# A causal mixer and a routed mixture of experts on one core: weight preparation, one token fetch and a scratch tile in another order

## The chip, the cores and the metric

One core of a Trainium2 chip runs the whole kernel in one launch. The metric is the time on the device in microseconds (us): the median of three runs, which lay between 1354.47 and 1360.31. The core has TensorE (PE in the rows; its weight loads are PEld), VectorE (DVE), ScalarE (ACT), GpSimd (POOL) and SyncE (SP), which issues most of the transfers.

## The reference

The input x has 8 sequences of 3584 tokens with 192 values. Two steps are computed.

```python
# 1. causal mixing: 8 heads of 24 values, 7 taps, the taps' softmax per head
out[b, s, h, :] = sum_k softmax(weight[h])[k] * x_pad[b, s + k, h, :]
# 2. each of the 28672 mixed tokens goes to one of 8 experts
logits = normalised(x) @ normalised(expert_emb).T / tau
expert = argmax(logits);  gate = softmax(logits)[expert]
y = gate * (relu(x @ w1[expert]) @ w2[expert])     # 192 -> 1024 -> 192
```

## The kernel before

**Chunks.** The tokens are worked on in 16 chunks of 1792 (112 partitions by 16 tiles), numbered 0 to 15 here. `mix` (line 405) does a chunk's mixing: eight fp32 matmuls with a band matrix, each copied back by ScalarE, and then the sum of squares of each of the 16 token tiles, three of four on ScalarE (line 425) and one on VectorE (line 428). Both write the squares themselves, which nobody reads, into tiles with the tag "sq", of which there are two. `route` (line 448) splits the chunk into fp16 high and low parts (lines 457 to 464), transposes it, makes the logits (line 496), finds expert and rank of each token on VectorE, and lists 16 scatters that write the chunk's rows into a table in DRAM, `rows_d`, sorted by expert. Chunks 0 and 1 are transposed by TensorE; from chunk 2 on this is done by DMA, 16 transposes per chunk in SyncE's queue (line 597, issued by `turn`).

**Weights.** `prep_load` (line 273) asks for one expert's fp32 weights, into one of three staging places in turn. Two of them lie in the buffers "slot" and "hid", which the expert blocks use later, the third in the last two experts' own images inside "res". `prep_weights` (line 292) is a generator with four steps per expert. Step 0 squares W1 by a Gram pass on TensorE (line 318) and takes its diagonal's sum on VectorE (line 323, into an "sq" tile). Step 1 does W2: for experts 0 to 3 another Gram pass, from expert 4 (BEHIND) on a square on ScalarE (line 309) whose result is thrown into the W2 part of the expert's own image. Step 2 sums both (line 328) and makes powers of two as scales. Step 3 splits the scaled weights into a high fp16 part on ScalarE (line 337) and a low one on VectorE (line 341). After each step some steps of chunks' work are taken from `dispatch` (HEAD: 2 each from expert 4 on). After an expert's step 3 the staging place is asked for again, for the third expert behind.

**Expert blocks.** When the counts of enough chunks are known (PICK: 2, 3, 4, 6, 9, 12), `hand_out` selects blocks of tokens of one expert with `select` (line 630), a chain of small VectorE steps that uses one "sl_ge" tile. Behind chunk 1 these are seven blocks of 256 tokens. `fetch` (line 710) reads the block's place into a SyncE register and issues a transposing load of its tokens (line 721) and a small one of its row numbers and gates (line 724). A fetch waits for the scatters of all chunks that were listed when its block was selected. `copy_w1` and `copy_w2` (lines 703, 706) copy the block's expert from "res" to "slot"; `expert` (line 754) does the block: 40 matmuls into "h_ps" (line 776), relu and its low part (lines 780, 782) into "hid", 24 matmuls per 128 tokens into "o_ps" (line 799), the gate (line 804) and a scatter to the output (line 806).

**Order.** SyncE's instructions run in the order in which they are written (a manual schedule). On the other engines a list scheduler places the instructions when the program is built, by a modelled time and with the written order as priority; manual dependencies hold some behind others. A tile whose tag has all its buffers in use waits for one. Before the main loop of `run` stand, in this order: the eight experts' preparation with HEAD steps between; 14 steps of `dispatch` (PRE); the first `hand_out`; three fetches; 8 more steps. The main loop then writes expert blocks, with steps of `dispatch` between by a planner's costs and due times.

Of the kernel before, what the change touches and what calls it, by code (L numbers as in the profile page):

```python
# [12 lines left out]
F16 = mybir.dt.float16  # L13
F32 = mybir.dt.float32
BF16 = mybir.dt.bfloat16
I32 = mybir.dt.int32
AF = mybir.ActivationFunctionType
# [8 lines left out]
D = 192  # L26
E = 8
F = 1024
HALO = 16
TP = 112  # L30
# [5 lines left out]
W2 = 3 * F  # L36
# [3 lines left out]
NFC = F // 128  # L40
# [4 lines left out]
BEHIND = 4  # L45
HEAD = 9, 8, 9, 4, 2, 2, 2, 2
# [21 lines left out]
def _dep(tc, frm, to, sync=True):  # L68
    cls = mybir.DependencyClass.Sync if sync else mybir.DependencyClass.NoSync
    tc.add_manual_dep(  # L70
        frm, to, mybir.DependencyInfo(cls, mybir.DependencyReason.DATA),
        reason="routed rows are written before they are read",
    )


class _Moe:
# [217 lines left out]
    def prep_weights(self, e, st):  # L294
        nc = self.nc
        img = self.res[:, e * RES:(e + 1) * RES]


        st, sw = st
        sr, sv = (v.bitcast(BF16).rearrange("p (n k) -> p n k", k=2)[:, :, 1]  # L300
                  for v in (st, sw))
        acc = self.sp.tile([128, 2], F32, tag="w_acc", name="w_acc")
        for k, cols in enumerate(
                ([(sr, 128, i) for i in range(NFC)]
                 + [(sr, 64, i) for i in range(NFC, 2 * NFC)],
                 [(sv, 128, i) for i in range(NFC * D // 128)])):
            if k and e >= BEHIND:

                i = nc.scalar.activation(
                    out=img[:, W2:W2 + NFC * D], in_=sw, func=AF.Square,  # L310
                    accum_out=acc[:, k:k + 1]).ins
                _dep(self.tc, i, self.act[1].name, False)
                yield
                continue
            tr = self.ps("h", [128, 128], F32, "tr_ps")
            for n, (v, rows, i) in enumerate(cols):
                v = v[0:rows, i * 128:(i + 1) * 128]
                i = nc.tensor.matmul(out=tr, lhsT=v, rhs=v, start=(n == 0),
                                     stop=(n == len(cols) - 1)).ins
                if e >= BEHIND:  # L320
                    _dep(self.tc, i, self.turned.name, False)
            dg = self.sp.tile([128, D], F32, tag="sq", name="w_dg")[:, 0:128]
            nc.vector.scalar_tensor_tensor(
                out=dg, in0=tr, scalar=1.0, in1=self.idf, op0=ALU.mult,
                op1=ALU.mult, accum_out=acc[:, k:k + 1])
            yield
        ps = self.ps("h", [128, 2], F32, "n2_ps")
        nc.tensor.matmul(out=ps, lhsT=self.onef, rhs=acc, start=True, stop=True)
        s, si = self.pow2(ps, [128, 2], 198, "w_p")
        s1, s2 = s[:, 0:1], s[:, 1:2]  # L330
        nc.vector.tensor_tensor(out=img[:, WS:WS + 2].bitcast(F32), in0=si[:, 0:1],
                                in1=si[:, 1:2], op=ALU.mult)
        yield
        xb = img[:, 2 * F:W2]
        b = img[:, W2:WS].rearrange("p (c d) -> p c d", d=2 * D)
        s_b = sw.rearrange("p (c d) -> p c d", d=D)
        hi = [nc.scalar.activation(out=o, in_=i, func=AF.Copy, scale=m).ins
              for o, i, m in ((img[:, 0:F], st[:, 0:F], s1),
                              (xb[0:64, :], st[0:64, F:2 * F], s1[0:64]),
                              (b[:, :, 0:D], s_b, s2))]  # L340
        lo = [nc.vector.scalar_tensor_tensor(
            out=o, in0=i, scalar=m, in1=h, op0=ALU.mult, op1=ALU.subtract).ins
              for o, i, m, h in (
                  (img[:, F:2 * F], st[:, 0:F], s1, img[:, 0:F]),
                  (xb[64:128, :], st[0:64, F:2 * F], s1[0:64], xb[0:64, :]),
                  (b[:, :, D:], s_b, s2, b[:, :, 0:D]))]
        if e >= BEHIND - 1:
            for i in hi:
                _dep(self.tc, i, self.act[e >= BEHIND].name, False)
        for i in lo:  # L350
            if e >= BEHIND - 2:
                _dep(self.tc, i, self.dve[e >= BEHIND].name, False)
            elif e:
                _dep(self.tc, i, self.cut.name, False)
        yield


    def load_x(self, c):
# [46 lines left out]
    def mix(self, c, ring, first):  # L405
        nc, sp = self.nc, self.sp

        yield _Gate(self.asked[c] + LAND_X)
        xt = self.xts[c]
        xc = xt[0:TP]  # L410
        for h in range(H):
            ps = self.ps(ring, [TP, NT, G], F32, "conv_ps")
            i = nc.tensor.matmul(out=ps, lhsT=self.band[:, h, :],  # L413
                                 rhs=xt[:, :, h * G:(h + 1) * G],
                                 start=True, stop=True).ins
            self.behind(i)
            self.clk += STEPC
            nc.scalar.copy(out=xc[:, :, h * G:(h + 1) * G], in_=ps)  # L418
            yield 0.0, 0.46

        n2 = sp.tile([TP, NT], F32, tag="n2", name="n2")
        for t in range(NT):
            sq = sp.tile([128, D], F32, tag="sq", name="sq")[0:TP, :]
            if t % 4 < NACT:
                nc.scalar.activation(out=sq, in_=xc[:, t, :], func=AF.Square,  # L425
                                     accum_out=n2[:, t:t + 1])
            else:
                nc.vector.scalar_tensor_tensor(  # L428
                    out=sq, in0=xc[:, t, :], scalar=1.0, in1=xc[:, t, :],
                    op0=ALU.mult, op1=ALU.mult, accum_out=n2[:, t:t + 1])  # L430
            if t % 2:
                yield ((0.54, 0.0), (0.27, 0.35), (0.0, 0.7))[
                    (t % 4 < NACT) + ((t - 1) % 4 < NACT)]
        s, si = self.pow2(n2[:], [TP, NT], 195, "x_p")
        y = self.rsqrt(n2[:], [TP, NT], "x_r")
        f = sp.tile([TP, NT], F32, tag="f", name="f")
        nc.vector.tensor_tensor(out=f, in0=n2, in1=y, op=ALU.mult)
        nc.vector.scalar_tensor_tensor(out=f, in0=f, scalar=1e-6, in1=s,
                                       op0=ALU.add, op1=ALU.mult)
        nc.vector.reciprocal(out=f, in_=f)  # L440
        nc.vector.tensor_scalar(out=f, in0=f, scalar1=self.rtau[:, 0:1],
                                scalar2=None, op0=ALU.mult)

        yield 1.5, 0.0
        self.mixed[c] = xc, s, si, f
# [460 lines left out]
    def run(self):  # L906
# [11 lines left out]
        st = self.conv_taps(w)  # L918
# [2 lines left out]
        self.nc.gpsimd.memset(self.onef, 1.0)  # L921
        first = min(PICK)
        a, spent = self.dispatch(first, "h"), [0.0, 0.0]
        for e in range(E):
            for _ in self.prep_weights(e, st[e]):
                for _ in range(HEAD[e]):
                    v = next(a, None)
                    if e >= BEHIND:
                        spent = [s + t for s, t in zip(spent, v)]
            if e + 3 < E:  # L930
                st.append(self.prep_load(e + 3))
            while self.later:
                self.load_x(self.later.pop(0))
            if e == BEHIND - 1:
                for _ in a:
                    pass
                a = self.dispatch(first, "r")
        self.weights_in = True
        for n in PRE:
            for _ in range(n):  # L940
                spent = [s + t for s, t in zip(spent, next(a))]
            if not self.subs:
                self.hand_out(first)
                while self.ready < min(3, len(self.subs)):
                    self.fetch()
        self.gated = True
        live, due, done, out = next(a, None), [0.0, 0.0], False, 0.0
        while live or self.pend or not done or self.at < len(self.subs):
            if self.at < len(self.subs):
                for v in self.expert():  # L950
                    self.steer(spent)
                    out = min(1.0, out + self.pace)
# [4 lines left out]
                    while live and min(due) >= 0.0:  # L957
# [6 lines left out]
                        spent = [s + t for s, t in zip(spent, live)]  # L964
# [29 lines left out]
```

## Time and profile before

| | |
|---|---|
| median of three runs | 1357.72 us |
| profiled execution | 1352.22 us |
| its span, first to last instruction | 1350.1 us |
| TensorE busy | 1188.8 us (88%) |
| VectorE busy | 835.1 us (62%) |
| ScalarE busy | 583.3 us (43%) |
| GpSimd busy | 543.7 us (40%) |
| mean granted TensorE clock | 0.941 |

A row of a timeline names its start and length in us, the engine (SPq is SyncE's queue), the line, the operation, what it writes and reads, how many instructions are merged in it, and in brackets how long the engine stood idle ahead of it and what ended that. "Issue" and "remote" mean that the profile shows no instruction it waited for.

### The profile page before, as it was taken

The page shows a single profiled execution, that of the slowest core. Times are in us where ns is not written, and L with a number is a line of the kernel's source. Part 1 is how long each engine was busy: PE and PEld are TensorE (multiplying, and loading weights), DVE is VectorE, ACT ScalarE, POOL GpSimd, SP SyncE. Part 2 cuts the span into 40 slices and gives each one's busy share as a digit, 9 for nine tenths or more (in the row PEclk, how much of TensorE's full clock was granted, in tenths as well). Part 3 has the DMA queues.
Part 4 walks back from the last instruction along what each step waited for, and adds up shares of the span by engine and source line. Part 5 has one row for each costly group of instructions (what it writes and reads, how often), then busy time and mean ns, then how long its engine had stood idle before and what let it go on. Part 6 is the DMA issues. An engine that isn't in the chain of part 4 may idle for free. (4 is left out here: it accounts for less than half of the span.)

```text
span 1350.1 us, 28933 instructions
## 1 busy us (share of the span) xinstructions
PE 1188.8 (88%) x10572; PEld 911.7 (68%) x10572; DVE 835.1 (62%) x2207; ACT 583.3 (43%) x1343; POOL 543.7 (40%) x541
## 2 busy tenths in 40 slices
PE   5673789897889998999888999889999999999998
PEld 3542578686776676767556667567777777799787
DVE  3967657667776756676676564635445555467475
ACT  4957344444534544544444533324333333333332
POOL 0064252455444546456445555663222222223232
PEclk9666789999899998999998999989999999999999
DMA  9473534536357444565446344312212121113120
GB/s 262 125 221 91 118 76 105 129 94 132 97 128 147 98 115 106 124 138 130 117 119 145 83 103 84 97 63 57 51 37 52 42 52 43 36 40 66 33 45 22
DMA packets 273950, 129.10 MB, mean 96 GB/s; under 512 B 215774, under 2 KB 264285, under 8 KB 273808
## 3 DMA queue, kind: packets, MB, share of 16 engines
q1 hardware_dynamic: 250000, 80.39, 28.2%
q0 software_dynamic: 23808, 46.87, 11.8%
q8 instruction: 83, 1.36, 0.4%
q14 instruction: 59, 0.48, 0.1%
HBM read 38.35 MB, written 47.53 MB: 64 GB/s over the span
## 5 line engine op out<-in xcount | busy, mean ns | idle before, releaser
L799 PE MATMUL o_ps<-slot,hid 128*128 128x192 f16 x5544 | 516.8, 250 | 68.4 <-issue 39.8
L799 PEld LDWEIGHTS <-hid 128*128 128x128 f16 x5544 | 467.4, 100 | 118.7 <-issue 65.8
L776 PE MATMUL h_ps<-e_xT,slot 128*128 128x256 f16 (+2 forms) x2944 | 502.3, 304 | 13.0 <-issue 8.2
L806 POOL DMA_INDIRECT out_dram<-y,e_mt x231 | 259.2, 1122 | 510.4 <-ACT y L804 464.6
L776 PEld LDWEIGHTS <-slot 128*128 128x128 f16 x3680 | 326.5, 99 | 202.4 <-issue 31.2
L782 DVE SCALAR_TENSOR_TENSOR hid<-h_ps,hid 128x512 f16<-128x512 f32 x462 | 309.6, 687 | 194.5 <-ACT hid L780 152.6
L780 ACT ACTIVATE hid<-h_ps 128x512 f16<-128x512 f32 x462 | 267.1, 598 | 236.3 <-PE h_ps L776 166.1
L601 POOL DMA_INDIRECT rows_d<-rows,di x256 | 266.9, 1042 | 222.6 <-issue 84.0
L804 ACT ACTIVATE y<-o_ps,g 128x192 f32<-128x192 f32 x231 | 95.4, 420 | 337.7 <-PE o_ps L799 260.8
L776 PE MATMUL h_ps<-e_xf,slot 128*128 128x256 f16 (+2 forms) x736 | 211.3, 303 | 2.0 <-issue 2.0
L706 DVE COPY slot<-res 128x3074 f16 x88 | 85.9, 976 | 162.4 <-PE o_ps L799 103.3
L413 PE MATMUL conv_ps<-xt,band 128*112 128x384 f32 x256 | 112.2, 545 | 19.0 <-ACT xt L418 7.9
L418 ACT COPY xt<-conv_ps 112x384 f32<-112x384 f32 x128 | 60.1, 480 | 73.9 <-PE conv_ps L413 54.1
L459 ACT CAST rows<-xt 112x768 f16<-112x768 f32 x64 | 52.9, 830 | 75.7 <-DMA rows_d<-rows,di 35.0
L703 DVE COPY slot<-res 128x3072 f16 x88 | 83.7, 952 | 0.0
L496 PEld LDWEIGHTS <-xT 128*112 128x112 f16 x768 | 58.7, 149 | 33.7 <-DMA xT<-rows 20.8
L496 PE MATMUL lg_ps<-ma,xT 128*112 128x16 f16 x512 | 57.9, 204 | 21.3 <-DMA xT<-rows 19.1
L413 PEld LDWEIGHTS conv_ps<-xt,band 128*112 128x112 f32 x256 | 43.2, 195 | 41.1 <-issue 20.5
L461 DVE TENSOR_TENSOR rows<-xt,rows 112x512 f16<-112x512 f32 x64 | 44.0, 687 | 40.5 <-ACT rows L459 30.9
L425 ACT ACTIVATE sq<-xt 112x192 f32<-112x192 f32 x192 | 67.8, 356 | 2.7 <-DVE sq L428 1.7
L457 DVE TENSOR_TENSOR xt<-xt,x_p_s 112x768 f32<-112x768 f32 x64 | 58.3, 952 | 0.2
L496 PE MATMUL lg_ps<-mb,xT 128*112 128x16 f16 x256 | 47.2, 206 | 1.9 <-ACT xT L492 1.4
(163 smaller groups left out, 528.7 us busy)
## 6 DMA issues: line engine op xcount, KB each, us to landing
xt<-in_dram SPq DMA_DIRECT2D x39, 384.0 KB
xt<-in_dram SPq DMA_DIRECT2D x3, 1440.0 KB
rows_d<-rows,di POOLq DMA_INDIRECT x256
res<-in_dram SPq DMA_DIRECT2D x5, 768.0 KB
out_dram<-y,e_mt POOLq DMA_INDIRECT x231
xT<-rows SPq DMA_TRANSPOSE x224
xt<-in_dram SPq DMA_DIRECT2D x2, 1536.0 KB
hid<-in_dram SPq DMA_DIRECT2D x3, 768.0 KB
```

The lines of the kernel that those rows point to most:

```text
L413: i = nc.tensor.matmul(out=ps, lhsT=self.band[:, h, :], rhs=xt[:, :, h * G:(h + 1) * G], start=True, stop=True).ins
L425: nc.scalar.activation(out=sq, in_=xc[:, t, :], func=AF.Square, accum_out=n2[:, t:t + 1])
L496: i = nc.tensor.matmul(out=lg[:, g * GX + a, :], lhsT=xT[:, a, k, :], rhs=self.mb if k == 1 else self.ma, start=(k == 0), stop=(k == 2)).ins
L601: i = self.nc.gpsimd.indirect_dma_start(out=self.rows_d[:, :], out_offset=bass.IndirectOffsetOnAxis(ap=idx, axis=0), in_=src, in_offset=No ...
L703: self.under(nc.vector.tensor_copy(out=self.slot[:, 0:W2], in_=v).ins)
L706: self.nc.vector.tensor_copy(out=self.slot[:, W2:], in_=self.res[:, bass.ds(self.we + W2, RES - W2)])
L776: self.mm = nc.tensor.matmul(out=ps[:, c, :], lhsT=w1(o, b + c), rhs=xk[k], start=(i == 0), stop=(i == 4)).ins
L780: self.step = nc.scalar.activation(out=hh[:, b:b + m, :], in_=ps, func=AF.Relu).ins
L782: self.low = nc.vector.scalar_tensor_tensor(out=hl[:, b:b + m, :], in0=ps, scalar=0.0, in1=hh[:, b:b + m, :], op0=ALU.max, op1=ALU.subtrac ...
L799: self.mm = nc.tensor.matmul(out=o, lhsT=h[:, c, q], rhs=w2[:, c, k:k + D], start=(c + i == 0), stop=(c == NFC - 1 and i == 2)).ins
L804: self.step = nc.scalar.activation(out=y, in_=o, func=AF.Copy, scale=g[:, a:a + 1]).ins
L806: i = nc.gpsimd.indirect_dma_start(out=self.out[:, :], out_offset=bass.IndirectOffsetOnAxis(ap=mt[:, a, 0:1], axis=0), in_=y, in_offset=No ...
```

## The change

The preparation's steps are put into a list and sorted: steps 0 and 1 of experts 5, 6 and 7 now stand ahead of step 3 of the expert before. Each still has its HEAD steps of `dispatch` behind it, so their number is the same, and so is the number of loads and their order. The first `hand_out` and one fetch stand ahead of the 14 steps, a second fetch ahead of the 8, and the third is written by the first `expert`. The square of W2 throws its result into a tile with the tag "xT" of the pool that block tokens use (three buffers). The products that VectorE throws away (the Gram diagonals and its share of the chunks' squares) go into a tile with the selection's tag "sl_ge"; the "sq" tiles are left to ScalarE.

```diff
@@ -307,7 +307,8 @@
             if k and e >= BEHIND:
 
                 i = nc.scalar.activation(
-                    out=img[:, W2:W2 + NFC * D], in_=sw, func=AF.Square,
+                    out=self.ep.tile([128, 3 * 512], F16, tag="xT", name="w_sq"),
+                    in_=sw, func=AF.Square,
                     accum_out=acc[:, k:k + 1]).ins
                 _dep(self.tc, i, self.act[1].name, False)
                 yield
@@ -319,7 +320,7 @@
                                      stop=(n == len(cols) - 1)).ins
                 if e >= BEHIND:
                     _dep(self.tc, i, self.turned.name, False)
-            dg = self.sp.tile([128, D], F32, tag="sq", name="w_dg")[:, 0:128]
+            dg = self.waste(128, 128)
             nc.vector.scalar_tensor_tensor(
                 out=dg, in0=tr, scalar=1.0, in1=self.idf, op0=ALU.mult,
                 op1=ALU.mult, accum_out=acc[:, k:k + 1])
@@ -355,6 +356,10 @@
         yield
 
 
+    def waste(self, p, n):
+        return self.lp.tile([128, D], F32, tag="sl_ge", name="waste")[0:p, 0:n]
+
+
     def load_x(self, c):
         nc = self.nc
         b, r0 = c // self.per_b, (c % self.per_b) * CT
@@ -420,13 +425,14 @@
 
         n2 = sp.tile([TP, NT], F32, tag="n2", name="n2")
         for t in range(NT):
-            sq = sp.tile([128, D], F32, tag="sq", name="sq")[0:TP, :]
             if t % 4 < NACT:
+                sq = sp.tile([128, D], F32, tag="sq", name="sq")[0:TP, :]
                 nc.scalar.activation(out=sq, in_=xc[:, t, :], func=AF.Square,
                                      accum_out=n2[:, t:t + 1])
             else:
                 nc.vector.scalar_tensor_tensor(
-                    out=sq, in0=xc[:, t, :], scalar=1.0, in1=xc[:, t, :],
+                    out=self.waste(TP, D), in0=xc[:, t, :], scalar=1.0,
+                    in1=xc[:, t, :],
                     op0=ALU.mult, op1=ALU.mult, accum_out=n2[:, t:t + 1])
             if t % 2:
                 yield ((0.54, 0.0), (0.27, 0.35), (0.0, 0.7))[
@@ -921,12 +927,20 @@
         self.nc.gpsimd.memset(self.onef, 1.0)
         first = min(PICK)
         a, spent = self.dispatch(first, "h"), [0.0, 0.0]
-        for e in range(E):
-            for _ in self.prep_weights(e, st[e]):
-                for _ in range(HEAD[e]):
-                    v = next(a, None)
-                    if e >= BEHIND:
-                        spent = [s + t for s, t in zip(spent, v)]
+        beats = [(e, k) for e in range(E) for k in range(4)]
+        beats.sort(key=lambda v: 4 * v[0] - 1.7 + v[1] * 0.3
+                   if v[0] > BEHIND and v[1] < 2 else 4 * v[0] + v[1])
+        gens = {}
+        for e, k in beats:
+            if not k:
+                gens[e] = self.prep_weights(e, st[e])
+            next(gens[e])
+            for _ in range(HEAD[e]):
+                v = next(a, None)
+                if e >= BEHIND:
+                    spent = [s + t for s, t in zip(spent, v)]
+            if k < 3:
+                continue
             if e + 3 < E:
                 st.append(self.prep_load(e + 3))
             while self.later:
@@ -936,13 +950,12 @@
                     pass
                 a = self.dispatch(first, "r")
         self.weights_in = True
+        self.hand_out(first)
         for n in PRE:
+            if self.ready < len(self.subs):
+                self.fetch()
             for _ in range(n):
                 spent = [s + t for s, t in zip(spent, next(a))]
-            if not self.subs:
-                self.hand_out(first)
-                while self.ready < min(3, len(self.subs)):
-                    self.fetch()
         self.gated = True
         live, due, done, out = next(a, None), [0.0, 0.0], False, 0.0
         while live or self.pend or not done or self.at < len(self.subs):
```

## Rows read from the trace of the kernel before

**Rows 1.** Four stretches: length, busy us per engine (instructions), clock, DMA share, GB/s.

```profile
100.00:120.00 20.00, 8.06 (x30) 4.15 (x30) 10.92 (x38) 13.35 (x44) 14.24 (x14) 0.78 0.33 104
120.00:150.00 30.00, 11.32 (x61) 8.07 (x62) 25.31 (x71) 16.05 (x27) 0.25 (x1) 0.50 0.48 106
...
165.00:175.00 10.00, 2.94 (x16) 1.25 (x15) 2.09 (x4) 0.60 (x1) 6.05 (x7) 0.70 0.66 148
175.00:250.00 75.00, 72.22 (x685) 62.60 (x684) 52.43 (x133) 34.15 (x83) 27.52 (x26) 0.95 0.36 85
```

**Rows 2.** TensorE's timeline, 100 to 192 us.

```profile
105.94 6.00 PE L413 MATMUL conv_ps<-xt,band 128*112 128x384 f32 x10 [4.93 <-ACT xt L418]
...
139.16 2.87 PE L413 MATMUL conv_ps<-xt,band 128*112 128x384 f32 x4 [6.24 <-DMA xt<-in_dram]
...
149.11 3.31 PE L776 MATMUL h_ps<-e_xT,slot 128*128 128x256 f16 x16 [2.51 <-DMA e_xT<-rows_d]
...
158.89 0.82 PE L776 MATMUL h_ps<-e_xT,slot 128*128 128x256 f16 x6
...
177.08 1.06 PE L776 MATMUL h_ps<-e_xT,slot 128*128 128x256 f16 x4
...
189.78 0.60 PE L776 MATMUL h_ps<-e_xT,slot 128*128 128x256 f16 x4
```

**Rows 3.** SyncE's queue, 120 to 170 us.

```profile
120.09 11.18 SPq L597 DMA_TRANSPOSE xT<-rows  x8
...
131.95 0.42 SPq L375 DMA_DIRECT2D xt<-in_dram  x1
132.49 12.07 SPq L597 DMA_TRANSPOSE xT<-rows  x8
146.06 1.23 SPq L721 DMA_TRANSPOSE e_xT<-rows_d  x1
...
151.31 1.22 SPq L721 DMA_TRANSPOSE e_xT<-rows_d  x1
...
164.33 0.51 SPq L375 DMA_DIRECT2D xt<-in_dram  x1
166.04 1.25 SPq L721 DMA_TRANSPOSE e_xT<-rows_d  x1
```

**Rows 4.** VectorE's timeline, 94 to 145 us.

```profile
96.28 0.20 DVE L654 TENSOR_TENSOR sl_ge<-sl_a,jf 1x56 f32<-1x56 f32 x1
...
103.96 0.16 DVE L677 CAST sel<-sl_ro 1x7 int32<-1x7 f32 x1
...
118.79 0.29 DVE L323 SCALAR_TENSOR_TENSOR w_dg<-tr_ps,idf 128x128 f32<-128x128 f32 x1 [3.36 <-remote]
...
121.11 0.35 DVE L428 SCALAR_TENSOR_TENSOR sq<-xt 112x192 f32<-112x192 f32 x1
...
128.23 0.35 DVE L428 SCALAR_TENSOR_TENSOR sq<-xt 112x192 f32<-112x192 f32 x1
...
142.24 0.95 DVE L703 COPY slot<-res 128x3072 f16 x1
```

**Rows 5.** Groups by line, 83 to 150 us: VectorE's split passes of two experts.

```profile
L341 DVE SCALAR_TENSOR_TENSOR res<-hid,w_p_s,res 128x1024 f16<-128x1024 f32 (+2 forms) x6 | 8.7, 1454 | 0.1
```

**Rows 6.** ScalarE's timeline: the squares of W2 of experts 6 and 7.

```profile
103.26 1.48 ACT L309 ACTIVATE res<-res 128x1536 f16<-128x1536 f32 x1 [3.20 <-DVE res L341]
...
128.26 1.48 ACT L309 ACTIVATE res<-hid 128x1536 f16<-128x1536 f32 x1 [0.94 <-DVE res L341]
```

**Rows 7.** GpSimd's timeline: the last scatter of chunk 1.

```profile
116.78 0.94 POOL L601 DMA_INDIRECT rows_d<-rows,di  x1 [0.30 <-issue]
```

**Rows 8.** Waits of VectorE, 150 to 900 us: total, times, longest.

```profile
DVE sq L428 <- ACT sq L425: 23.6, 17, 6.3
```

**Rows 9.** Waits of TensorE, 150 to 900 us.

```profile
PE o_ps L799 <- DVE hid L782: 6.9, 11, 2.1
PE lg_ps L496 <- DMA xT<-rows: 2.3, 3, 1.3
```

## The prediction, written before the changed kernel ran

> **What bounds the kernel now.** I read the busy time by stretch first [rows 1]. From 175 us on TensorE sets the time: 72.2 of 75 us busy in 175 to 250, and the page's slices behind 850 us show it at 9 tenths. Not so at the front: from 100 to 150 TensorE works 19.4 of 50 us, at a granted clock of 0.78 and then 0.50 (its lower level, 1.2 GHz), while VectorE works 10.9 of 20 and then 25.3 of 30. From 165 to 175 nobody works (TensorE 2.9 of 10), with the DMA engines 66% busy.
>
> Next TensorE's timeline, for what ends its idle time at the front [rows 2]: the mixing matmuls wait 4.93 us for ScalarE, the mixing of chunk 4 6.24 us for its x, and the first expert block starts at 149.11 after 2.51 us for its own tokens. Block 0 then takes 9.8 us (149.11 to 158.89), block 1 18.2 (to 177.08), block 2 12.7 (to 189.78).
>
> Why the tokens come so late is seen in SyncE's queue, which runs in the order written [rows 3]: 16 transposes of chunk 2 with a load of x between them occupy it from 120.09 to 144.56, and only then stand the three fetches, the first at 146.06 and the last at 151.31. Data is there 3.05 us after an issue (146.06 to 149.11). The slot copy of block 0's weights needs every weight in its place; it starts at 142.24, behind the last split pass of expert 7 [rows 4]. So two things hold block 0, at 142 and at 149, and the queue is the later.
>
> **The change, part by part.**
>
> *Squares and Gram passes ahead of the split.* Before, the square of W2 threw its result into the expert's own image. For experts 6 and 7 that memory is another expert's staging, so ScalarE's queue stood 3.20 us at 103.26 and 0.94 us at 128.26 until VectorE's split had read it [rows 6]. Behind the first of these stood the copies that TensorE waited 4.93 us for. The diagonal of expert 7's Gram pass waited 3.36 us on VectorE, until 118.79 [rows 4]; the passes of ScalarE's squares just ahead of it use the same two "sq" tiles, and I take that as the reason. Nothing is added: the same Gram passes, squares of 1.48 us and three VectorE split passes of 1.454 on the mean, 4.4 us per expert [rows 5], stand in another order. What is moved is VectorE's: in 100 to 120 it idles 9.1 of 20 us [rows 1]. Earliest end of expert 7's split: behind expert 5's last pass, which let ScalarE go on at 103.26, two splits of 4.4, eight squares of 0.35 and an estimated 20 small steps of 0.16 (as the one at 103.96), 118. Latest: where it is, 142.3. I take 121, nearer to the early end, because the waits that held its links, 3.36 and 0.94 us and all that queued behind them, are the ones that go.
>
> What is pushed back for it? Chunk 2's subtractions, whose first rows started the transposes at 120.09. VectorE has 8.8 us of splits more ahead of them and 9.1 us of idle time to put them in. I leave their start where it is, at 120 (bounds 117, if only the 3.36 us goes, and 126, if half of the idle time stays).
>
> *The first fetch ahead of the transposes.* It needs the selection, which was complete at 103.96 [rows 4], and the scatters of chunks 0 and 1, whose last issue is at 116.78 and lasts 0.94 [rows 7]; their landing isn't in the rows. With the 3 us that a token fetch takes as the upper bound and nothing as the lower, the fetch is issued between 117.7 and 121; I take 120.5. Its tokens are there at 123.5, behind expert 7's split, and block 0 runs from 124 to 134 in time that TensorE idles now. A fetch takes 2.6 us of the queue (two in 146.06 to 151.31), so the transposes start at 123 instead of 120.09 and last the same 24.5 us, to 147.5. Fetch 1 goes out at 149.0 (the step from last transpose to fetch was 1.5), its tokens are there at 152, and block 1 starts at 152 where it started at 158.89: 6.9 us sooner, not the 25 by which block 0 is.
>
> Fetch 2 now stands behind chunk 3's eight transposes and the load of chunk 5. That stretch of queue took 14.7 us (151.31 to 166.04), so it goes out at 163.7. Block 1 gets block 0's old 9.8 us and ends at 162. Block 2 starts at 167 to 171 (3 us behind the issue, or when the load of 1.5 MB is through, which took 7.2 us at 131.95 to 139.16); I take 169, against 177.08: 8 us. In the old run the load of chunk 5 at 164.33 fell on block 1's second half: in 165 to 175 TensorE, VectorE and ScalarE all stood [rows 1], and block 1 took 8.4 us more than block 0. It now falls where TensorE waits for fetch 2 anyway.
>
> Order in one queue decides between 167 and 171, and no row here shows it: tokens fetched right behind the load of chunk 5 were not used until long after. The Trainium skill, DMA: Bandwidth & Descriptors, section "Two DMAs through the same engine are not ordered", says that within one queue of an engine descriptors start in order; by it block 2 would start at 171 and the gain would be 6, without it 10.
>
> Block 0 paid for a cold TensorE: its first 16 matmuls took 3.31 us after a stretch at clock 0.50. The same four matmuls took 1.06 us at 177.08, behind the standstill, and 0.60 at full clock, at 189.78 [rows 2], so 16 cold ones lose about 1.8. The change opens a second such gap, from 134 to 152, so block 1 pays 1.8 us too; that is in the 9.8 I gave it. The Trainium skill, TensorE: Matmul & The Clock Gate, section "Part 1: The HAM clock gate", says that throttled is the default and activity releases it, which speaks against running one block alone; if block 1 kept its clock, the gain would be 1.8 more.
>
> *Own tile for VectorE's squares.* In 150 to 900 VectorE stood 23.6 us in 17 pieces for ScalarE's squares, and TensorE 6.9 us for VectorE's hid [rows 8, 9]. These share only little: bounds 0 and 6.9, and I take 1, since VectorE is busy 70% of 175 to 250 and catches up. The tile is the selection's "sl_ge", of which there is one, so squares and selections now follow one another in it. All of it is VectorE's own, which needs no wait; but a selection can't run before squares written ahead of it.
>
> *Sum.* 8 from the front and 1 from the tile. From 175 on the work is the same, TensorE-bound, and what waits there is not for tokens or transposes (2.3 us in 750 for the logits [rows 9], none named for block tokens), so I carry it to the end: 1352.2 - 9 = 1343 for a profiled execution. The profiled one before lies 5.5 us under the median of its runs (1357.72), so the time is 1348.5. Likeliest case's own range: gains of 4 to 15, 1343 to 1354.
>
> **Rivals.**
>
> *A, larger:* transposes start at 117, since the diagonal's wait goes, and block 1 starts at 149 with its full clock; block 2 follows at 164. Gain 13 at block 2 and up to 4 more from VectorE's squares, 17: 1341. For it: all three waits are long and removed. Against it: the scatters hold the first fetch to 117.7 at the least.
>
> *B, nothing:* block 0 isn't taken out of its place. The order on TensorE is fixed when the program is built; chunk 4's mixing stood there in front of ready logits and made them wait 6.24 us. If block 0's matmuls stand behind the logits of chunk 2 again, it starts at 148 to 150, block 1 follows at 158, and fetch 2, 12 us later than before, holds block 2 to 169 or more, so what is left is the stretch around 165: gain 0 to 4, 1356. For it: that row. Against it: the tokens are there 20 us before the last logits.
>
> *C, slower:* the first fetch blocks SyncE. The selection can't take its one tile before chunk 3's squares; three of them were written ahead of it and ran between 121.11 and 128.23 [rows 4]. If they stay there, the selection ends at 128.6 plus the 7.7 us from its comparison to its result (96.28 to 103.96), the fetch is issued at 137 and the transposes start at 139.5, 19 us late. By the steps above block 1 then starts at 168.5, fetch 2 goes out at 180, and block 2 starts at 183 to 187, 8 us later than before: 1366. Block 2 is no later than before as long as the first fetch leaves by 129; from there each us costs one. Against it: these squares move up with expert 6's and 7's steps.
>
> **How the numbers follow.** Forecast 0.47, A 0.14, B 0.24, C 0.15. What a measurement here can tell from no change is about 0.5%, 6.8 us: faster means under 1350.9. Of the forecast I count 0.37 there and 0.10 within; A wholly faster; B 0.01 faster, 0.21 within and 0.02 slower; C 0.02 within and 0.13 slower. Faster 0.52, same 0.33, slower 0.15. Range: down to 1337 for what lies beyond A's low end, and up to 1361, which leaves C's worst out.
>
> **What would show it.** Right: the first token fetch ahead of the first row transpose, near 120; ScalarE's second W2 square without a wait; expert 7's split over by 125; block 0 starting near 124 and block 1 near 152, with TensorE at half clock between; block 2 near 169. Wrong: SyncE idle at its first fetch until after 125 (C); block 0 at 148 or later (B); block 2 at 169 but the distance lost by 900 us, which would mean that the stalls in the middle are not fixed costs.

## The result: 1.1% slower, and where the time went

The changed kernel took 1369.53 us (median of 6 runs, 1367.16 to 1374.21) beside 1355.9 for the one before on the same chip: ratio 1.0108, 95% interval 1.0081 to 1.0134. Its profiled execution took 1370.0 us, span 1368.1, granted clock 0.932. The forecast was 1348.5.

SyncE's queue of the changed kernel, 120 to 176 us (start, duration, instruction, count), to be held against [rows 3]:

```profile
130.04 1.34 SPq L727 DMA_TRANSPOSE e_xT<-rows_d  x1
...
132.15 11.45 SPq L603 DMA_TRANSPOSE xT<-rows  x8
...
144.81 11.76 SPq L603 DMA_TRANSPOSE xT<-rows  x8
157.37 1.24 SPq L727 DMA_TRANSPOSE e_xT<-rows_d  x1
...
159.98 1.25 SPq L727 DMA_TRANSPOSE e_xT<-rows_d  x1
...
162.04 12.02 SPq L603 DMA_TRANSPOSE xT<-rows  x8
174.18 0.51 SPq L380 DMA_DIRECT2D xt<-in_dram  x1
175.57 1.27 SPq L727 DMA_TRANSPOSE e_xT<-rows_d  x1
```

The first fetch leaves at 130.04, not 120.5, and everything written behind it on SyncE is late: chunk 2's transposes start 12.06 us later (132.15 against 120.09), and the fetch behind chunk 3's transposes and the load of x leaves at 175.57 instead of 166.04.

VectorE's timeline of the changed kernel, 113 to 130 us, against [rows 4]; the ends of the lines say what each writes and reads:

```profile
117.21 2.59 DVE L342 SCALAR_TENSOR_TENSOR res<-hid,w_p_s,res 128x1024 f16<-128x1024 f32 x2
...
119.92 1.81 DVE L342 SCALAR_TENSOR_TENSOR res<-hid,w_p_s,res 128x1536 f16<-128x1536 f32 x1
121.65 0.68 DVE L467 TENSOR_TENSOR rows<-xt,rows 112x512 f16<-112x512 f32 x1
...
126.28 0.36 DVE L433 SCALAR_TENSOR_TENSOR waste<-xt 112x192 f32<-112x192 f32 x1
...
126.71 0.11 DVE L659 MEMSET sl_ge<- 1x63 f32 x1
...
126.86 0.20 DVE L660 TENSOR_TENSOR sl_ge<-sl_a,jf 1x56 f32<-1x56 f32 x1
...
128.70 0.10 DVE L683 CAST sel<-sl_ro 1x7 int32<-1x7 f32 x1
```

The reader sees two things. The selection's comparison, at 96.28 before, starts at 126.86, directly behind the third of chunk 3's squares (126.28) in the same one tile; the selection is complete at 128.70 and the fetch leaves 1.34 us later. And expert 7's split (117.21 to 121.7) now stands ahead of chunk 2's first subtraction (121.65), which frees the first transposes. That subtraction was at 119.01 before, so of the 12.06 us the rows are 2.64, the selection 7.31 (the transposes began 1.08 behind the first subtraction before, so they could have begun at 122.73; the fetch leaves at 130.04) and the fetch itself 2.11 (130.04 to 132.15). The scatters are not what held the fetch: the last of them is issued at 119.61, and in e10 below a fetch leaves 2.6 us behind that point.

TensorE's timeline of the changed kernel, and its busy time in the stretches of [rows 1] (columns as there):

```profile
133.19 3.57 PE L782 MATMUL h_ps<-e_xT,slot 128*128 128x256 f16 x16 [14.21 <-DMA e_xT<-rows_d]
...
160.45 3.57 PE L782 MATMUL h_ps<-e_xT,slot 128*128 128x256 f16 x16 [2.41 <-DMA e_xT<-rows_d]
...
184.38 0.82 PE L805 MATMUL o_ps<-slot,hid 128*128 128x192 f16 x4 [5.52 <-issue]
```

```profile
120.00:150.00 30.00, 12.06 (x112) 10.35 (x112) 25.10 (x80) 11.79 (x36) 3.59 (x5) 0.71 0.33 82
165.00:175.00 10.00, 10.00 (x107) 9.38 (x106) 8.57 (x29) 4.33 (x8) 2.56 (x3) 1.00 0.45 77
175.00:250.00 75.00, 59.68 (x569) 50.80 (x567) 43.65 (x113) 28.05 (x71) 29.66 (x30) 0.89 0.40 93
```

Block 0 does run out of its place, at 133.19 instead of 149.11, but block 1 starts at 160.45 instead of 158.89. The standstill that was at 165 to 175 is now behind the later load of x: TensorE's pieces put down to "issue" add to 13.2 us from 178 to 194 (5.52 the longest), where they were 7.0 from 165 to 175 before. In 175 to 250 TensorE is busy 12.5 us less than before [rows 1].

To follow the loss I use the start of VectorE's gate step, one per expert block (`g<-e_mt,slot`). After minus before, in us: block 0 -12.0, block 1 +0.8, block 2 -5.5, block 3 +8.4, block 6 +8.2, block 36 +10.1, block 42 +19.8, last block +18.2. So 8 us are lost by block 3, and some 10 more between blocks 36 and 42. In that second stretch TensorE's waits for VectorE add to 9.7 us after and 2.9 before, and it is busy 5.1 us longer; what makes VectorE late there stays open.

### The profile page after: what moved, and what is told of

The parts are those of the page before. It is cut to its first block, busy times and chain, and to the rows that moved or that the text cites. A ratio compares the mean times of both kernels' runs of the same rounds, so it can differ in the third digit from the quotient of the medians.

```text
span 1368.1 us, 28953 instructions
## 1 busy us (share of the span) xinstructions
PE 1199.3 (88%) x10572; PEld 914.6 (67%) x10572; DVE 840.0 (61%) x2207; ACT 578.4 (42%) x1343; POOL 550.1 (40%) x541
## 5 line engine op out<-in xcount | busy, mean ns | idle before, releaser
L607 POOL DMA_INDIRECT rows_d<-rows,di x256 | 272.9, 1066 | 213.3 <-issue 103.1
L418 PE MATMUL conv_ps<-xt,band 128*112 128x384 f32 x256 | 117.7, 567 | 17.3 <-ACT xt L423 7.4
```

The costliest lines, as they stand in the source:

```text
L418: i = nc.tensor.matmul(out=ps, lhsT=self.band[:, h, :], rhs=xt[:, :, h * G:(h + 1) * G], start=True, stop=True).ins
L607: i = self.nc.gpsimd.indirect_dma_start(out=self.rows_d[:, :], out_offset=bass.IndirectOffsetOnAxis(ap=idx, axis=0), in_=src, in_offset=No ...
```

## Experiments

They ran on several chips. The kernel before took 1344.7 us beside e1 to e4 and 1267 us beside all the others; each result is the ratio to the kernel before on the same chip, with its 95% interval. "Selection" is the start of its last step, "transposes" that of chunk 2's first one. T is the theory "the late selection holds SyncE".

**e1: a tile of its own for VectorE's squares** (half precision; nothing else uses it), else as after.

```diff
-        return self.lp.tile([128, D], F32, tag="sl_ge", name="waste")[0:p, 0:n]
+        return self.lp.tile([128, D], F16, tag="waste", name="waste")[0:p, 0:n]
```

> The changed kernel, but VectorE's thrown-away products go to an fp16 tile with a tag of its own instead of the selection's tile. Theory T (the selection stands behind chunk 3's squares in the one shared tile, so the first fetch left at 130.0 and held SyncE's transposes by 12 us): selection over by 112, first fetch issued at 118 to 122, transposes from 121 to 124, block 1 at 151 to 154; total 0.988 to 1.000 of before. Rival R1 (the fetch ahead of the transposes is itself the loss: queue time, cold TensorE, fetch 2 behind the load): block 1 early, but the total stays over 1.005. Rival R2 (the splits put ahead push chunk 2's rows back): transposes not before 126, total 1.004 to 1.010. Rival R3 (VectorE's squares without the shared sq tiles cost the middle): front 6 us early, 10 us lost between 600 and 900, total 1.003 to 1.010.

Measured 1.0041 (1.0012 to 1.0070). The selection is complete at 104.32 and the fetch leaves at 122.30, yet the transposes start only at 126.98. Both signs of R2 come true (transposes not before 126, 1.004 to 1.010). VectorE shows why: chunk 2's first subtraction stands behind the copy of the first fetched tokens, and that copy waits for them.

```profile
125.41 0.46 DVE L749 COPY e_xf<-e_xT 64x256 f16<-64x256 f16 x2 [6.86 <-DMA e_xT<-rows_d]
125.88 0.69 DVE L467 TENSOR_TENSOR rows<-xt,rows 112x512 f16<-112x512 f32 x1
```

The ratio is about 0.7% lower than the change's, each known to 0.3%, but the time isn't under before, so T isn't all.

**e2: the squares back in the two shared "sq" tiles**, else as after.

```diff
-        return self.lp.tile([128, D], F32, tag="sl_ge", name="waste")[0:p, 0:n]
+        return self.sp.tile([128, D], F32, tag="sq", name="waste")[0:p, 0:n]
```

> The changed kernel with VectorE's thrown-away products in the two sq tiles that ScalarE uses, as before; reordering and early fetch kept. T: selection free, first fetch at 118 to 122; transposes from 121 to 126 (the sq tiles may hold a Gram diagonal again for 1 to 3 us); total 0.990 to 1.003 of before. R1: over 1.005. R3: better than the kernel with an own tile by 5 us or more, since the middle is as before.

Measured 1.0096 (1.0057 to 1.0136). Selection 104.08, fetch 118.33, close to the scatters' bound that the forecast named; transposes at 133.47, since chunk 2's first subtraction comes at 132.38, behind the splits of experts 6 and 7. T alone falls: with the selection in time, something else is as late. R3 falls too, as this is no better than e1.

**e3: fetches late**, else as after (one tile "sl_ge", new order).

```diff
-        self.hand_out(first)
         for n in PRE:
-            if self.ready < len(self.subs):
-                self.fetch()
...
+            if not self.subs:
+                self.hand_out(first)
+                while self.ready < min(3, len(self.subs)):
+                    self.fetch()
```

> The changed kernel with the selection and all three fetches behind the 14 steps, as before; reordering and shared sl_ge tile kept. T: the late selection (about 128) holds nobody, since the fetches stand behind the transposes; these start at 121 to 123 when the rows are there, first fetch at 147 to 149, block 0 at 150 to 152; total 0.997 to 1.005 of before, so 9 us or more better than the changed kernel. R1: the same. R2 and R3: 1.006 to 1.011, as the changed kernel, since the reordering and the tile are still there.

Measured 1.0074 (1.0036 to 1.0112). The selection is as late as in the changed kernel (129.90) and holds nobody; transposes at 123.93. The new order and the tile cost 0.7% without any fetch ahead, as R2 and R3 had it (1.006 to 1.011).

**e4: the fetch alone**: before, with the first fetch ahead as in the change (the diff of e3 turned round).

> The kernel before with only the selection and fetches put ahead. T: the selection is over at 104, so the first fetch leaves at 118 to 122, transposes from 121 to 124, but expert 7's split still ends at 142, so block 0 starts at 143 to 147 and block 1 at 152 to 156; total 0.993 to 1.002 of before. R1: over 1.005, like the changed kernel.

Measured 1.0011 (0.9982 to 1.0039). Fetch 121.30, transposes 123.39, block 0 no sooner (its last split ends at 147). Moved alone it is worth nothing and costs nothing that can be measured, so R1 falls.

**e5: the shared tile alone**: before, with the squares and diagonals of VectorE in "sl_ge" (this part of the change's diff).

> Before, with one edit: VectorE's squares and the diagonal products write into the one sl_ge tile that the selection also uses; splits and fetches keep the old order. T (the harm is SyncE standing at a first fetch whose selection is late): the fetches stand behind chunk 2's transposes here, so a late selection holds nobody; the selection may end as late as 129, fetch 0 stays near 146, and the time is within 0.3% of before. R (the tile itself serialises VectorE's squares or pushes ScalarE's wait elsewhere, over the whole kernel): 0.4 to 0.8% slower, with the loss spread between 200 and 900 us.

Measured 1.0060 (1.0042 to 1.0078). T's 0.3% is missed. The selection is late by the tile alone (121.44, against 96.66 in the kernel before on this kind of chip) and holds nobody. The ratio is in R's range, but its profile doesn't show the spread that R named (2.3 us late at block 6, 3.3 at the end).

**e6: the order alone**: the change's `beats` and W2 squares; squares in "sq", fetches late.

> Before, with the order of Gram passes, W2 squares and splits changed, and nothing else: the squares stay in the two sq tiles, the fetches stay behind 14 steps. O (the reordering pushes chunk 2's rows back): transposes start at 123 to 130 instead of 120, block 1 2 to 6 us later than before, the time 0.3 to 0.8% slower. T alone (only the late selection harms): selection near 104, transposes near 120, the time within 0.3% of before or up to 0.3% faster.

Measured 1.0088 (1.0060 to 1.0116): nearly the whole loss, without tile or fetch. O has the direction, and more than its 0.8%.

**e7: the own tile alone** (e1's tile, old order and fetches).

> Before, with VectorE's squares and diagonal products in a tile of their own (half precision, since a full one finds no room), which nothing else uses; old order of splits and fetches. If the waits of VectorE on ScalarE's squares (23.6 us in the trace of before) cost anything, this is 0.1 to 0.5% faster than before; if they only move to the next step, the norm's first product, it is within 0.2% of before, and those waits are found there instead.

Measured 1.0050 (1.0030 to 1.0069), slower than both expectations. Here, too, a split has come ahead of chunk 2's rows, though the written order of the steps is the old one; expert 6's split and the first subtraction:

```profile
104.01 1.28 DVE L341 SCALAR_TENSOR_TENSOR res<-slot,w_p_s,res 128x1024 f16<-128x1024 f32 x1 [1.38 <-ACT res L337]
...
112.64 0.68 DVE L466 TENSOR_TENSOR rows<-xt,rows 112x512 f16<-112x512 f32 x1
```

In the kernel before on this kind of chip (c1 below) that split starts at 112.28, behind the subtraction at 107.58. In e5 it is the same: split at 101.63, subtraction at 110.43. So a change of scratch tile alone was enough for the list scheduler to place the split otherwise.

**e8: three fetches ahead**: e1 with

```diff
-            if self.ready < len(self.subs):
+            while self.ready < min(3, len(self.subs)):
```

> After, with the squares in a tile of their own and all three fetches ahead of chunk 2's transposes, where after has one. If TensorE's idle stretch of 134 to 152 can be filled by blocks 1 and 2: block 1 at 135 to 145 and block 2 by 160, transposes 5 us later than with one fetch ahead, and the time 0 to 0.8% under the version with one fetch ahead (1.0041 of before), so 0.996 to 1.004 of before. If the transposes' delay decides: each us of theirs is given back at the logits of chunk 2 and the time is 1.005 or more.

Measured 1.0047 (1.0029 to 1.0066), as e1, between the two expectations. Transposes at 129.34; VectorE stands 8.21 us for fetched tokens ahead of chunk 2's first subtraction (125.13).

**c1 and c2: before and after, unchanged, on the faster kind of chip.**

> The kernel before, unchanged, for a profile beside those of its variants on the same chip. On the chip of the tile-alone run the kernel before took 1267 us where the first chip took 1350. If that is the chip, the difference is in TensorE's idle time that the profile puts down to nothing (issue, 39.8 us at the second expert product on the first chip) and in the granted clock, with the same order of instructions; if it is an order that varies, block starts differ from the first trace by more than a common drift.

> The changed kernel, unchanged, beside the one before on this chip. T: the first token fetch 8 to 12 us later than chunk 2's rows would allow, whatever the chip; ratio 1.005 to 1.013. If the loss needed the first chip's slow stretches between 690 and 890 us, the ratio here is 1.002 to 1.006 and block by block the distance stays level behind the eighth block.

Measured: c1 span 1265.8 us; c2 1.0107 (1.0074 to 1.0141), the same ratio as on the first chip, as T had it. TensorE, ScalarE, GpSimd and SyncE ran the same instructions in the same order in c1 as in the first chip's trace, so c1's first case holds: the difference is the chip's, not another order. The distance is +14.8 us at block 6 and +22.4 at the end; the profiled c2 (1289.8 us) is the slowest of its runs, and the medians lie 14.6 apart. VectorE of c1, then of c2:

```profile
107.58 0.70 DVE L461 TENSOR_TENSOR rows<-xt,rows 112x512 f16<-112x512 f32 x1
...
112.28 1.28 DVE L341 SCALAR_TENSOR_TENSOR res<-slot,w_p_s,res 128x1024 f16<-128x1024 f32 x1
...
126.20 1.28 DVE L341 SCALAR_TENSOR_TENSOR res<-hid,w_p_s,res 128x1024 f16<-128x1024 f32 x1
```

```profile
109.13 2.60 DVE L342 SCALAR_TENSOR_TENSOR res<-slot,w_p_s,res 128x1024 f16<-128x1024 f32 x2 [0.86 <-ACT res L338]
...
117.53 2.59 DVE L342 SCALAR_TENSOR_TENSOR res<-hid,w_p_s,res 128x1024 f16<-128x1024 f32 x2
...
121.97 0.68 DVE L467 TENSOR_TENSOR rows<-xt,rows 112x512 f16<-112x512 f32 x1
```

Before, chunk 2's subtractions run ahead of the splits of expert 6 (`slot`) and 7 (`hid`); after, behind both. That is 14.4 us here and was 2.64 on the first chip, because there the kernel before was itself late at this point (119.01); the changed one is not (121.65 and 121.97). The transposes start at 108.67 and 132.46: 14.4 for the rows, 7.3 for the selection, 2.1 for the fetch.

**e9: the place of W2's square alone.**

```diff
-                    out=img[:, W2:W2 + NFC * D], in_=sw, func=AF.Square,
+                    out=self.ep.tile([128, 3 * 512], F16, tag="xT", name="w_sq"),
+                    in_=sw, func=AF.Square,
```

> Before, with one edit: the squares of W2 go into a tile of the tokens' kind instead of the expert's own image; old order, old tiles, old fetches. P (ScalarE's waits of 3.20 and 0.94 us behind the split are what holds the front): ScalarE goes on 3 us sooner behind 103, chunk 2's rows and so the transposes start 1 to 3 us sooner, and the time is 0 to 0.3% under before. S (the new tile is one of a pair of tokens' tiles and its square holds back the logits' tiles, or the static order of VectorE shifts as with every edit so far): transposes no sooner and the time 0.2 to 0.9% over before.

Measured 0.9984 (0.9965 to 1.0003), transposes at 106.61, 2.06 us sooner than c1. P's transposes come true; its gain is at the edge of what can be told, as the interval takes in 1.

**e10: fetch ahead and own tile, old order.**

> Before, with two parts of the change and without the new order of splits: first fetch ahead of chunk 2's transposes, and VectorE's squares in a tile of their own. If the parts add up (fetch alone 1.0011, own tile alone 1.0050), the ratio is 1.004 to 1.008. If the own tile's loss is a front effect that an early fetch takes back, as in the version with all three (1.0041), it is 0.999 to 1.004.

Measured 1.0070 (1.0042 to 1.0097): the parts add up. Its VectorE shows a third thing ahead of chunk 2's rows, the copy of the first fetched tokens:

```profile
121.91 0.22 DVE L748 COPY e_xf<-e_xT 64x256 f16<-64x256 f16 x1 [13.88 <-DMA e_xT<-rows_d]
...
126.25 0.68 DVE L466 TENSOR_TENSOR rows<-xt,rows 112x512 f16<-112x512 f32 x1
```

The fetch left at 118.79, 2.6 us behind the start of the last scatter (116.17), so VectorE stood from 108 to 121.9 with the scaling of chunk 2 queued behind the copy. It is the wait of e1 (6.86 us) and e8 (8.21); e4 has it too (5.18), behind the first subtraction.

**e11: the splits pinned behind the rows.** e6, with the last step of experts 6 and 7 written behind chunk 2's rows and ordered behind them, on VectorE (shown) and likewise on ScalarE; no wait is added that an engine's own order doesn't give.

```diff
+            if e > 5 and k == 3:
+                self.held.append(gens[e])
...
-                _dep(self.tc, i, self.dve[e >= BEHIND].name, False)
+                _dep(self.tc, i, (self.cut if e > 5 else
+                                  self.dve[e >= BEHIND]).name, False)
```

> The new order of Gram passes and W2 squares, squares in the two sq tiles, fetches late (as in the order-alone run), and one edit: the splits of experts 6 and 7, on VectorE and ScalarE, stand behind chunk 2's rows. V (the order loses because these splits stand ahead of chunk 2's rows on VectorE, 10 us of them): chunk 2's first subtraction 9 to 11 us sooner than in the order-alone run, where the ratio was 1.0088, and the ratio here 0.996 to 1.001. W (the order loses by the Gram passes and squares themselves, or in blocks further on): ratio 1.005 or more.

Measured 0.9997 (0.9978 to 1.0015). First subtraction 108.11, transposes 109.18, against 117.80 and 118.88 in e6. VectorE of e6, then of e11:

```profile
113.35 2.59 DVE L342 SCALAR_TENSOR_TENSOR res<-hid,w_p_s,res 128x1024 f16<-128x1024 f32 x2
...
117.80 0.68 DVE L467 TENSOR_TENSOR rows<-xt,rows 112x512 f16<-112x512 f32 x1
```

```profile
108.11 0.68 DVE L470 TENSOR_TENSOR rows<-xt,rows 112x512 f16<-112x512 f32 x1
...
112.59 2.58 DVE L343 SCALAR_TENSOR_TENSOR res<-slot,w_p_s,res 128x1024 f16<-128x1024 f32 x2
```

V holds and W falls: pinning the two splits takes the 0.88% back.

**e12: the same with the own tile.**

> The run before this with VectorE's squares in a tile of their own. Own tile alone was 1.0050 with chunk 2's first subtraction 5 us late, behind expert 6's split. V: with the splits behind the rows the tile costs nothing: ratio 0.995 to 1.001, and if the waits on ScalarE's squares were worth anything it is under the run with sq tiles. If the tile itself costs (waits moved to the norm's first step in the middle of the kernel): 0.3 to 0.6% over the run with sq tiles.

Measured 1.0028 (1.0009 to 1.0046): 0.3% over e11, the tile's second case. First subtraction 110.80, 2.7 us behind e11's. VectorE's waits from 150 to 900 us in e11 and in e12 (total, times, longest):

```profile
DVE waste L436 <- ACT sq L433: 25.5, 19, 5.8
```

```profile
DVE waste L436 <- ACT xt L426: 10.0, 6, 3.3
DVE x_p_e L154 <- ACT sq L433: 9.2, 4, 3.3
```

25.5 us of waits for ScalarE's squares became 19.2: 10.0 for ScalarE's copies of x and 9.2 at the norm's first step.

**e13: the first fetch between the halves of the transposes**: e9, with the fetch behind chunk 2's first eight transposes and the load, and its copies ordered behind chunk 2's rows.

```diff
                 self.load_x(c + 2)
+                if c == min(PICK):
+                    self.hand_out(c)
+                    self.fetch()
...
+            if not self.flips:
+                _dep(self.tc, v, self.rows_in.name, False)
```

> Before, with W2's squares in a tokens' tile (alone 0.9984) and the first fetch between the two halves of chunk 2's transposes, its flip copies behind chunk 2's rows; old order otherwise. My forecast's mechanism without its two obstacles: selection and scatters are through by then, so the queue loses only the fetch's 2.6 us; block 0 runs 8 to 14 us sooner in time that TensorE idles, block 1 starts 5 to 8 us sooner: ratio 0.992 to 0.997. If block 0 ahead is worth nothing (the queue's 2.6 us and a second slow start of TensorE eat it): 0.998 to 1.003.

Measured 0.9977 (0.9961 to 0.9992), the best of all and 3 us under before, but only 0.07% under e9. It lies between the two ranges named, next to the one in which block 0 ahead is worth nothing.

**e14: e11 and e13 together.**

> The new order with splits behind chunk 2's rows and squares in sq tiles, and the first fetch between the halves of the transposes: the change with what held the rows and the queue taken away. V: like the run before this or up to 0.2% under it, 0.990 to 0.997. If the order adds a cost of its own: 0.3% or more over the run before this.

Measured 0.9999 (0.9982 to 1.0017): 0.2% over e13, less than the 0.3% named, and out of V's range; no gain from the new order.

The profiled runs beside 1267 us in one table (three chips, on which the kernel before took 1267.0, 1267.9 and 1267.2 us); the last two columns are the gate step of block 1 and block 6 minus c1's, in us:

| run | first subtraction | transposes start | block 1 | block 6 | ratio |
|---|---|---|---|---|---|
| c1 before | 107.58 | 108.67 | 0 | 0 | 1 |
| e9 square's place | 105.52 | 106.61 | -1.2 | +2.3 | 0.9984 |
| e13 fetch between | 105.56 | 106.64 | -6.3 | -1.0 | 0.9977 |
| e14 both | 108.22 | 109.30 | -3.7 | -1.1 | 0.9999 |
| e11 rows first | 108.11 | 109.18 | +1.4 | 0.0 | 0.9997 |
| e12 rows first, own tile | 110.80 | 111.88 | +3.9 | +2.7 | 1.0028 |
| e5 shared tile | 110.43 | 111.51 | +3.7 | +2.3 | 1.0060 |
| e7 own tile | 112.64 | 113.73 | +6.0 | +6.0 | 1.0050 |
| e6 order | 117.80 | 118.88 | +12.3 | +10.9 | 1.0088 |
| e10 fetch, own tile | 126.25 | 127.34 | +9.0 | +9.2 | 1.0070 |
| e8 three ahead | 125.13 | 129.34 | +9.4 | +7.9 | 1.0047 |
| c2 after | 121.97 | 132.46 | +13.3 | +14.8 | 1.0107 |

Without a fetch ahead, a later start of the transposes is later at block 6 by about as much (e6: 10.2 and 10.9), and block 6 in 1267 us is about the ratio (10.9 is 0.86%). With fetches ahead 9 to 13 us come back (e10: 18.7 late, 9.2 lost; e8: 20.7 and 7.9). Two rows don't fit. e5's profiled run (1271.0 us) is the fastest of its runs and shows 2.3 us where the ratio is 7.6; e9's (1269.46) is the slowest of its runs, 2.3 us late at block 6 though its transposes start 2.06 sooner. The parts alone (e4 0.11, e5 0.60, e6 0.88) add to more than the 1.08% of the change, as expert 6's split ahead of chunk 2's rows is in both e5 and e6.

## Why the prediction was wrong

*The step that failed: "It needs the selection, which was complete at 103.96".* I took a time of the old order for the new one, though the change put the selection and the squares in one tile. The comparison waited for squares written ahead of it, and the fetch left at 130.04, not 120.5. This is rival C's obstacle, to which I gave 0.15, in its place: e1 takes the shared tile away and brings the selection to 104.32. C's path from there to its number was another, and its sizes were off. I added 7.7 us from comparison to result, where it took 1.84 (126.86 to 128.70): in the old run those steps stood between other work. And I let the loss begin at a fetch later than 129, where a fetch at 130.04 came with a loss of 1.1%. And C had its 8 us lost at block 2: that block's gate step came 5.5 us sooner, and the 8 us show at block 3, behind the longer standstill (13.2 us against 7.0). C's 1366 against 1369.5 is therefore luck in part.

*"I leave their start where it is, at 120".* Wrong, and the larger half on the second chip. I counted the 8.8 us of splits put ahead into VectorE's 9.1 idle us [rows 1], with a bound of 126. Idle time of a whole stretch isn't idle time ahead of the one instruction that is waited for: the splits went into the queue ahead of the rows, together with the waits of their own inputs (2.06 us for the norm of the weights in e6). e6 and e11 show it: chunk 2's rows 10 us late with them ahead, and on time without.

*A third thing, which the sum put at nothing:* the copy of the fetched tokens on VectorE. In e1, e4, e8 and e10, where the selection is in time, VectorE stands 5.18 to 13.88 us for these tokens while chunk 2's rows queue behind. The forecast let the transposes start one fetch (2.6 us) later and had no such wait.

*What was right:* expert 7's split over at 121.7 (121 forecast); its W2 square waits no longer on a split (`104.30` waits 1.74 us for a load instead); the diagonal's 3.36 us gone, though that the "sq" tiles were its reason isn't shown (in c1, with these tiles, the diagonal doesn't wait either); block 0 out of its place, so rival B falls; a second cold start, 3.57 us for block 1's first 16 matmuls. TensorE had done nothing in 119 to 133 (granted clock 0.50, its lower level of 1.2 GHz), and in 158 to 160.4 it was at 0.50 again with 0.03 us of work; over 160.4 to 164, block 1's first matmuls, the clock was still 0.50. The Trainium skill, TensorE: Matmul & The Clock Gate, section "Part 1: The HAM clock gate", says that the throttled clock is the default; the trace agrees here, in those three stretches.

*Fetch 2* does not stand behind chunk 3's transposes, as I had it, but right behind fetch 1 (159.98); it is the next one, block 3's, that stands there (175.57). So no run here tells whether its tokens land behind the load ahead of it, which I weighed for block 2.

*"From 175 on the work is the same, so I carry it to the end."* The gain in the front was real in mechanism: e13, without the two obstacles, has blocks 1 and 2 6.3 and 6.8 us sooner, close to the 6.9 and 8 forecast. But at block 3 it is 3.1 and at block 6 1.0. TensorE's timeline of e13 shows the places:

```profile
166.53 4.27 PE L808 MATMUL o_ps<-slot,hid 128*128 128x192 f16 x46 [0.81 <-DVE hid L791]
...
178.46 1.33 PE L808 MATMUL o_ps<-slot,hid 128*128 128x192 f16 x14 [2.08 <-DVE hid L791]
...
181.15 4.66 PE L808 MATMUL o_ps<-slot,hid 128*128 128x192 f16 x28 [1.36 <-DVE hid L791]
```

These waits for VectorE add to 4.3 us in 150 to 200 where c1 has 2.6, and TensorE's clock in 175 to 250 is 0.93 against 0.98. So part of the gain went in waits for a VectorE that was no sooner, and part in the clock; I had noted VectorE busy 70% of 175 to 250 and read it as slack. e13 ran only on the faster kind of chip, where the standstill at 165 to 175, on which part of block 2's 8 us rested, doesn't occur (TensorE is busy all of 150 to 175 in c1); what it gives on the first kind isn't shown.

*The tile's gain of 1* isn't there: alone 1.0050. The waits moved to the norm's first step and to the copies of x, as e12's rows show. In e7 expert 6's split, 4.4 us, stands ahead of rows that are 5 us late; with the splits pinned (e12) 2.7 us at the front remain.

*Open:* the 10 us that the first pair lost between blocks 36 and 42, which the second pair doesn't show (there the last 8 go between blocks 9 and 28); e5's missing 0.4%; and the 2.7 us of e12, which are there already at expert 5's last split pass (99.08 against 95.06 in e11).

## What to carry to other kernels

When a step is moved ahead in a queue, every input of it needs its time in the *new* order; a tile with one buffer puts its users into the order in which they were written, however short they are. When a wait is removed, the work that it held back takes a place in front of somebody: find the instruction that the next queue waits for and pin the freed work behind it (pinning two splits was worth 0.88%). A changed scratch tile can be enough to move that work, with the written order untouched (e5, e7). And follow a gain over the next blocks: 6.8 us at block 2 were 1.0 at block 6.

## What the runs showed of the hardware

The same kernel's span was 1350.1 us on the first chip and 1265.8 on another, at granted clocks of 0.941 and 0.961. The page's group of the second expert product, with its idle time and what ended most of it, before on the first chip, then on the other:

```profile
L799 PE MATMUL o_ps<-slot,hid 128*128 128x192 f16 x5544 | 516.8, 250 | 68.4 <-issue 39.8
```

```profile
L799 PE MATMUL o_ps<-slot,hid 128*128 128x192 f16 x5544 | 495.8, 247 | 34.9 <-DVE hid L782 21.8
```

On the first chip TensorE stands 39.8 us ahead of these matmuls for nothing that the profile shows, 7.0 of it right behind the load of x (165 to 175 in before) and 13.2 behind the same load in after (178 to 194); on the other chip TensorE is busy 25.0 of 25 us in 150 to 175. The ratio of the two kernels is the same on both, and so is the order of TensorE's instructions. What differs between the chips, no run here shows.
